# Spreading the last tokens and v over the DMA engines, row sums on the full array, and unread products in gaps

## The chip, the cores and the metric

The kernel runs on one core of a Trainium2 chip. The metric is the time of one execution on the device in microseconds (us), the median of several runs. The core has a matrix engine (TensorE, PE in the profile; its weight loads are listed apart as PEld), VectorE (DVE), ScalarE (ACT), GpSimd (POOL), a sync engine (SP) that issues most transfers, and 16 DMA engines that carry them out.

## The reference

Attention over keys and values that are averaged in groups of eight, and a mixing MLP on its output. Sizes: 8 batches, 8 heads, 576 tokens, 64 values per head; so the model width is 512 and there are 72 pooled keys; the hidden width is 2048.

```python
k_p = k.reshape(B, H, 72, 8, 64).mean(axis=3)
v_p = v.reshape(B, H, 72, 8, 64).mean(axis=3)
attn = softmax(q @ k_p.T / 8)                     # 576 x 72 for each batch and head
x = heads side by side of (attn @ v_p)            # B x 576 x 512

a1 = alpha1 * x + beta1
u = x + lam * einsum('ts,bsd->btd', w_tok, a1)    # mixes tokens
a2 = alpha2 * u + beta2
out = u + lam * (maximum(a2 @ w_ch1, 0) @ w_ch2)
```

The 576 tokens are four chunks of 128 and a rest of 64, called rem below. Because alpha1, beta1 and lam don't depend on the token, beta1 enters the mix as lam * beta1 times the sum of each row of w_tok; the kernel computes these row sums and puts them into one extra row of the transposed w_tok.

## The kernel before

The work is one program in which every engine has its own queue of instructions in the order written. A start computes batch 0's attention and mix; then come nine blocks of 512 tokens of the MLP, with the attention and mix of the next batch woven between their matmuls.

The loads. A rem transfer brings two rows of 64 values for 128 partitions, from four heads (every second one) times 32 pairs of tokens:

```python
def load_rem(b, queue=nc.sync):
    raw = work.tile([P, 2, 2, 2, D], FP, tag="rem_raw", bufs=2, name="rem_raw")
    for i, src in enumerate((q, k)):
        for h in range(2):
            queue.dma_start(
                out=raw[:, i, h].rearrange("p c d -> p (c d)"),
                in_=src[b, h::2, 512:576, :].rearrange("a (i c) d -> a i (c d)", c=2))

def load_v(b, hp):
    v_hp = work.tile([SPG, 2, 8, D], FP, tag="v_hp", bufs=4, name="v_hp")      # SPG = 72
    nc.sync.dma_start(out=v_hp.rearrange("g h p d -> g h (p d)"),
                      in_=v[b, 2 * hp:2 * hp + 2].rearrange("h (g p) d -> g h (p d)", p=8))
```

The transposed w_tok and its row sums. The last of the five products of a row sum has only 64 rows:

```python
def setup_wtok(tcx, copy):
    ...                                        # five transposes on PE
    copy(out=wtT[:, 0:5, P * tcx:P * tcx + trc], in_=...)      # ScalarE

def setup_rowsum(tcx):
    ...
    for sc in range(5):
        kk = P if sc < 4 else 64
        nc.tensor.matmul(out=ps[:, 0:trc], lhsT=ones_bf[0:kk], rhs=wtT[0:kk, sc, cols],
                         start=(sc == 0), stop=(sc == 4))
    nc.scalar.copy(out=wtT[64:65, 4, cols], in_=ps[64:65, 0:trc])
```

Helpers that the order below names:

```python
def setup_vectors():       # one transpose of beta2, and a copy by ScalarE
def setup_bias(g):         # 16 products of w_ch1 with beta2, one column each, and a copy by ScalarE
def keep_warm(count):      # products that nothing reads
    ps = gp("ps_warm")
    for _ in range(count):
        nc.tensor.matmul(out=ps, lhsT=identity_bf, rhs=warm)
def mix_T(b, c, eng):      # 5 products of 512 columns, then u = x + product (VectorE),
                           # then u_bf = u * alpha2 (VectorE or GpSimd)
def mix_uT(key):           # 4 transposes of u_bf on PE, then a copy by ScalarE to u_fm
def mlp_A(n, j):           # 4 products of w_ch1 with u_fm, then relu by ScalarE
```

The start of the program, cut (att_F transposes q, att_K pools k on PE, att_V sums v on VectorE, S are scores and exponentials, AV the products with v, att_X scales x for the mix):

```python
load_qk(0, 0)
...                        # small vectors on ScalarE's queue: lam, alpha1, alpha2, beta1, lam, beta2
load_v(0, 0)
load_qk(0, 2)
load_rem(0)
load_v(0, 2)
load_qk(0, 1); load_v(0, 1); load_qk(0, 3); load_v(0, 3)
...
broadcast(0, lam_bc)       # one row to 128 partitions, a float32 product on PE
sum_k(0, 0, nc.gpsimd)
cast_q(0, 0, nc.vector.tensor_copy)
att_F(0, 0)
broadcast(1, lamal_bc, by=lam_bc)
att_V(0, 0)
sum_k(0, 2, nc.gpsimd)
cast_q(0, 2, nc.scalar.copy)
nc.vector.tensor_tensor(out=lamb1, in0=b1row, in1=lamrow, op=ALU.mult)
att_F(0, 2)
...
broadcast(2, al2_bc)
cast_rem(0, nc.gpsimd, nc.vector.tensor_copy)
att_Frem(0, (0,), nc.vector.tensor_copy)
att_K(0, 0, nc.vector.tensor_copy)
att_V(0, 2)
pro_S(0)
pro_S(2)
...                        # w_tok, w_ch1 and w_ch2 are loaded; the other two pairs of heads
setup_wtok(0, nc.scalar.copy)
setup_wtok(1, nc.scalar.copy)
att_X(0, 2, 4, eng=nc.gpsimd)
pro_AV(3)
setup_wtok(2, nc.scalar.copy)
setup_rowsum(0)
setup_rowsum(1)
setup_wtok(3, nc.scalar.copy)
att_X(0, 6, 8)
setup_rowsum(2)
setup_rowsum(3)
mix_T(0, 0, nc.gpsimd)
mix_T(0, 1)
mix_T(0, 2, nc.gpsimd)
mix_uT((0, 0))
mix_T(0, 3)
mix_uT((0, 1))
...                        # loads of batch 1
setup_vectors()
setup_bias(0)
mix_uT((0, 2))
keep_warm(1)
mix_uT((0, 3))
...                        # blocks: mlp_A, mlp_B, and the next batch between
```

Of the kernel before, what the change touches and what calls it, by code (L numbers as in the profile page):

```python
# [9 lines left out]
BF = mybir.dt.bfloat16  # L10
AF = mybir.ActivationFunctionType
ALU = mybir.AluOpType
AX = mybir.AxisListType

P = 128
# [8 lines left out]
def kernel(  # L24
# [59 lines left out]
# [4 lines that stand above are left out]
            for h in range(2):  # L88
                queue.dma_start(
                    out=raw[:, i, h].rearrange("p c d -> p (c d)"),  # L90
                    in_=src[b, h::2, 512:576, :].rearrange("a (i c) d -> a i (c d)", c=2))
        st1[b]["rem_raw"] = raw

    def load_v(b, hp):
        v_hp = work.tile([SPG, 2, 8, D], FP, tag="v_hp", bufs=4, name="v_hp")
        nc.sync.dma_start(out=v_hp.rearrange("g h p d -> g h (p d)"),
                          in_=v[b, 2 * hp:2 * hp + 2].rearrange("h (g p) d -> g h (p d)", p=8))
        st1[b]["v"][hp] = v_hp

    def cast_rem(b, eng, copy=None):  # L100
        raw = st1[b]["rem_raw"]
        rq = work.tile([P, 2, 2, D], BF, tag="rem_q", bufs=2, name="rem_q")
        rk = work.tile([P, 2, D], BF, tag="rem_k", bufs=2, name="rem_k")
        (copy or eng.tensor_copy)(out=rq.rearrange("p c h d -> p h c d"), in_=raw[:, 0])  # L104
        eng.tensor_tensor(out=rk, in0=raw[:, 1, :, 0], in1=raw[:, 1, :, 1], op=ALU.add)
        st1[b]["rem"] = rq, rk
# [45 lines left out]
    for t, src in ((b1row, moe_beta1), (lamrow, moe_lam)):  # L152
# [16 lines left out]
    ones_bf = const.tile([P, P], BF, tag="ones_bf", name="ones_bf")  # L169
    nc.vector.memset(identity_bf, 0.0)  # L170
    nc.vector.memset(pool_main, 0.125)
    nc.vector.memset(pool_rem, 0.125)
    nc.vector.memset(identity, 0.0)
    nc.gpsimd.affine_select(out=identity_bf, in_=identity_bf, compare_op=ALU.not_equal,
                            fill=1.0, base=0, pattern=[[-1, P]], channel_multiplier=1)
    for t, n, width in ((pool_main, 64, 2), (pool_rem, 32, 4)):
        nc.gpsimd.affine_select(out=t, in_=t, compare_op=ALU.is_ge, fill=0.0, base=0,
                                pattern=[[-width, n]], channel_multiplier=1)
        nc.gpsimd.affine_select(out=t, in_=t, compare_op=ALU.is_ge, fill=0.0, base=width - 1,
                                pattern=[[width, n]], channel_multiplier=-1)  # L180
    nc.gpsimd.affine_select(out=identity, in_=identity, compare_op=ALU.not_equal,
                            fill=1.0, base=0, pattern=[[-1, P]], channel_multiplier=1)
    nc.vector.memset(ones_bf, 1.0)

    vp1_pool, kpT_pool, ET_pool = [], [], []
    for i in range(4):
# [18 lines left out]

    wtT = const.tile([P, 6, 640], BF, tag="wtT", name="wtT")
    nc.vector.memset(wtT[:, :, S:640], 0.0)

    def broadcast(i, out, by=None):

        ps = gp("ps_bc")
        nc.tensor.matmul(out=ps, lhsT=ones_row, rhs=vecs[:, i])
        if by is None:
            nc.scalar.copy(out=out, in_=ps)
        else:
            nc.vector.tensor_tensor(out=out, in0=by, in1=ps, op=ALU.mult)
# [6 lines left out]
    def setup_wtok(tcx, copy):  # L223

        trc = P if tcx < 4 else REM
        w = wt_bf[0:trc, S * tcx:S * tcx + 640]
        strided = w[:, 0:512].rearrange("p (m c) -> p c m", c=4)
        ps_w = gp("ps_w").bitcast(BF)
        for sc in range(5):
            nc.tensor.transpose(out=ps_w[0:P, trc * sc:trc * sc + trc],  # L230
                                in_=strided[:, sc, :] if sc < 4 else w[:, 512:640],
                                identity=identity_bf[0:trc, 0:trc])
        copy(out=wtT[:, 0:5, P * tcx:P * tcx + trc],
             in_=ps_w[:, 0:5 * trc].rearrange("p (s t) -> p s t", t=trc))

    def setup_rowsum(tcx):

        trc = P if tcx < 4 else REM
        cols = slice(P * tcx, P * tcx + trc)
        ps = gp("ps_rs")  # L240
        for sc in range(5):
            kk = P if sc < 4 else 64
            nc.tensor.matmul(out=ps[:, 0:trc], lhsT=ones_bf[0:kk], rhs=wtT[0:kk, sc, cols],
                             start=(sc == 0), stop=(sc == 4))
        nc.scalar.copy(out=wtT[64:65, 4, cols], in_=ps[64:65, 0:trc])

    def setup_wtok_odd():
# [56 lines left out]
    def att_Frem(b, us, copy):  # L304

        st = st1[b]
        if "ps_qr" not in st:
            ps_q = gp("ps_qr").bitcast(BF)
            for c in range(2):
                nc.tensor.transpose(out=ps_q[:, 128 * c:128 * c + 128],  # L310
                                    in_=st["rem"][0][:, c].rearrange("p h d -> p (h d)"),
                                    identity=identity_bf)
            st["ps_qr"] = ps_q
        for u in us:
            copy(out=st["qT"][u][:, 512:640].rearrange("p (r i c) -> p r c i", r=2, c=2),
                 in_=st["ps_qr"][:, 0:256].rearrange("p (c r u i) -> p u r c i", c=2, r=2,
                                                     u=2)[:, u])

    def att_K(b, u, copy):

        st = st1[b]
        ps_kp = gp("ps_kp")
        kp = ps_kp[:, 0:2 * SPG].rearrange("p (r g) -> p r g", g=SPG)
        for r in range(2):
            nc.tensor.matmul(out=kp[:, r, 0:64],
                             lhsT=st["k"][u + 2 * r].rearrange("p h d -> p (h d)"), rhs=pool_main)
        nc.tensor.matmul(out=kp[:, :, 64:72], lhsT=st["rem"][1].rearrange("p h d -> p (h d)"),  # L327
                         rhs=pool_rem.rearrange("p (r u g) -> p u r g", u=2, g=8)[:, u])
        for hh in range(2):
            rows = slice(64 * hh, 64 * hh + 64)  # L330
            copy(out=kpT_pool[u][rows, hh], in_=kp[rows])  # L331
# [44 lines left out]
    def att_X(b, h0, h1, groups=1, eng=nc.vector):  # L376

        x, xs = st1[b]["x"], xs_pool[b % 2]
        for h in range(h0, h0 + 4 * groups, 4):
            cols = slice(D * h, D * (h + h1 - h0))  # L380
            eng.tensor_tensor(  # L381
                out=xs[:, 0:4, cols], in0=x[:, 0:4, cols],
                in1=lamal_bc[:, cols].unsqueeze(1).to_broadcast((P, 4, D * (h1 - h0))),
                op=ALU.mult)
        p0 = 64 * (b % 2)
        for h in range(h0, h0 + 4 * groups, 4):
            cols = slice(D * h, D * (h + h1 - h0))
            eng.tensor_tensor(out=xs[p0:p0 + 64, 4, cols], in0=x[p0:p0 + 64, 4, cols],  # L388
                                    in1=lamal_bc[p0:p0 + 64, cols], op=ALU.mult)
# [20 lines left out]
    def mix_T(b, c, eng=nc.vector):  # L410
        key, s = chunk_of(b, c)
        p0, p1 = (0, P) if c < 4 else (64 * (b % 2), 64 * (b % 2) + 64)
        xs = xs_pool[b % 2]
        ps_tok = gp("ps_tok")
        t0 = P * c - 64 * (b % 2) if c == 4 else P * c
        for sc in range(5):
            kk, at = (P, sc) if sc < 4 else (P, 5) if b % 2 else (65, 4)
            nc.tensor.matmul(out=ps_tok, lhsT=wtT[0:kk, at, t0:t0 + P],  # L418
                             rhs=xs[0:kk, sc, :], start=(sc == 0), stop=(sc == 4))
        nc.vector.tensor_tensor(out=s["u"][p0:p1, :], in0=st1[b]["x"][p0:p1, c, :],  # L420
                                in1=ps_tok[p0:p1, 0:DM], op=ALU.add)
        eng.tensor_tensor(out=s["u_bf"][p0:p1, :], in0=s["u"][p0:p1, :],  # L422
                          in1=al2_bc[p0:p1, :], op=ALU.mult)
# [54 lines left out]
    def pro_AV(hp):  # L478
        att_AV(0, 2 * hp)
        att_AV(0, 2 * hp + 1)  # L480
# [12 lines left out]
    for i, p0 in ((0, 64), (1, 0)):  # L493
        nc.scalar.copy(out=xs_pool[i][p0:p0 + 1, 4, :], in_=lamb1[p0:p0 + 1, :])
    broadcast(2, al2_bc)
    cast_rem(0, nc.gpsimd, nc.vector.tensor_copy)
    att_Frem(0, (0,), nc.vector.tensor_copy)
    att_K(0, 0, nc.vector.tensor_copy)
# [27 lines left out]
    setup_wtok(0, nc.scalar.copy)  # L526
    setup_wtok(1, nc.scalar.copy)
    att_X(0, 2, 4, eng=nc.gpsimd)
    pro_AV(3)
    setup_wtok(2, nc.scalar.copy)  # L530
    setup_rowsum(0)
    setup_rowsum(1)
    setup_wtok(3, nc.scalar.copy)
    att_X(0, 6, 8)
    setup_rowsum(2)
    setup_rowsum(3)
    mix_T(0, 0, nc.gpsimd)
    mix_T(0, 1)
    mix_T(0, 2, nc.gpsimd)
    mix_uT((0, 0))  # L540
    mix_T(0, 3)
# [6 lines left out]
    for hp in (1, 3):  # L548
        load_qk(1, hp)
        load_v(1, hp)  # L550
    setup_vectors()
    setup_bias(0)
    mix_uT((0, 2))
    keep_warm(1)
    mix_uT((0, 3))


    def attention(b):
# [89 lines left out]
```

The softmax here doesn't subtract the row's maximum and nothing guards it: scores larger than these inputs give would overflow.

## Time and profile before

| what | value |
|---|---|
| time, median of 3 runs | 385.42 us (384.75 to 386.6) |
| profiled execution | span 384.7 us, 5969 instructions |
| data moved | 43.01 MB in 34307 packets |
| sync queue, share of 16 DMA engines | 34.7% |
| v, per transfer | 288 KB, 32 transfers |
| q, k, per transfer | 256 KB, 32 transfers each |
| rem of q and of k, per transfer | 64 KB, 16 transfers each |
| w_tok | 576 KB and 72 KB as kept, landed 5.8 and 6.0 us after issue |
| first score product | 14.97 us |
| first mix product | 31.98 us |
| first large MLP product | 41.10 us |

The page of a profile lists busy times of the engines, then the span in 40 equal slices (each digit the busy share in tenths), the DMA queues, and the chain of work that ended last, followed back from the end. Finer answers from the same trace are used below: the chain of waits in order of time (start, length, what), the instructions of one engine in order of time (start, length, engine and line, operation, operands, how many, and in brackets the idle time before and what ended it), and stretches of time with the busy time of every engine. L89 is line 89 of the kernel.

### The profile page before, as it was taken

To read this page: it belongs to the slowest core of one execution; us is meant where nothing else is said; L and a number is where in the kernel's file an instruction comes from. 1 tells how busy PE (TensorE), PEld (TensorE's weight loads), DVE (VectorE), ACT (ScalarE), POOL (GpSimd) and SP (SyncE) were. 2 spreads that over 40 slices of the span, in tenths; PEclk is the share of its full clock that TensorE was granted. 3 is DMA by queue.
4 is the path that set the end of the run, shared out by engine and by line. 5 is a ranking of instruction groups with operands and counts; after the bars stand their busy time and mean duration, and the time that the engine had idled before them with its cause. 6 is when DMAs were issued, how large, how long until landed. Compare 5 with 4: busy or idle time off the path is not lost.

```text
span 384.7 us, 5969 instructions
## 1 busy us (share of the span) xinstructions
PE 358.4 (93%) x2221; PEld 193.9 (50%) x2263; DVE 219.0 (57%) x464; ACT 191.2 (50%) x383; POOL 81.8 (21%) x133
## 2 busy tenths in 40 slices
PE   6579899879999999999999999999999999999995
PEld 2265455435554555445545554455555544544542
DVE  6394809975577457755776578637863685011011
ACT  3462468416951595148605860487138713722710
POOL 4372246610350044004400360035000000000000
PEclk9999899999999999999999999999999999999999
DMA  5799995803951195118511861076110001002012
GB/s 154 212 176 216 220 243 147 250 28 120 223 137 57 57 238 130 55 45 219 162 55 36 229 163 54 30 213 173 41 54 1 23 34 55 1 27 83 0 42 67
DMA packets 34307, 43.01 MB, mean 112 GB/s; under 512 B 2331, under 2 KB 23903, under 8 KB 34278
## 3 DMA queue, kind: packets, MB, share of 16 engines
q1 hardware_dynamic: 31872, 37.76, 34.7%
q0 software_dynamic: 2384, 4.86, 6.8%
q8 instruction: 17, 0.28, 0.3%
q14 instruction: 12, 0.10, 0.1%
q10 hardware_dynamic: 22, 0.02, 0.0%
HBM read 38.04 MB, written 9.44 MB: 123 GB/s over the span
## 4 chain that ended last, share of the span: by engine, by line
PE 79%; DVE 14%; DMA 3%; ACT 2%; issue 1%; SPq 1%; POOL 0%; ACTq 0%; POOLq 0%
PE ps_h L444 33%; PE ps_ch L460 23%; PE ps_tok L418 12%; DVE x_tm L373 4%; DVE xs L381 3%; PE ps_sc L349 3%; PE ps_uT L433 2%; PE ps_q L297 2%; DMA v_hp<-in_v_dram 1%; DMA rem_raw<-in_k_dram 1%; PE ps_av L365 1%; DVE xs L388 1%; DVE rec L371 1%; DVE u_sb L465 1%; ACT ET L351 1%
## 5 line engine op out<-in xcount | busy, mean ns | idle before, releaser
L460 PE MATMUL ps_ch<-w,Hj 128*128 128x512 bf16 x555 | 137.8, 379 | 1.0
L444 PE MATMUL ps_h<-u_fm,w 128*128 128x512 bf16 x558 | 132.6, 383 | 1.7 <-ACT u_fm L435 0.7
L447 ACT ACTIVATE Hj<-ps_h,bias_cols 128x512 bf16<-128x512 f32 x144 | 99.1, 689 | 41.6 <-PE ps_h L444 41.2
L444 PEld LDWEIGHTS <-w 128*128 128x128 bf16 x576 | 63.6, 115 | 52.8 <-issue 3.1
L460 PEld LDWEIGHTS <-Hj 128*128 128x128 bf16 x576 | 54.4, 98 | 48.9
L435 ACT COPY u_fm<-ps_uT 128x512 bf16<-128x512 bf16 x36 | 21.0, 586 | 95.9 <-PE ps_uT L433 95.8
L351 ACT ACTIVATE ET<-ps_sc 72x288 f16<-72x288 f32 x128 | 44.6, 405 | 25.9 <-PE ps_sc L349 25.2
L418 PE MATMUL ps_tok<-xs,wtT 128*128 128x512 bf16 (+1 forms) x197 | 50.3, 386 | 4.1 <-DVE xs L381 3.7
L465 DVE TENSOR_TENSOR u_sb<-u_sb,ps_ch 128x512 f32<-128x512 f32 x36 | 24.5, 682 | 50.6 <-PE ps_ch L460 50.2
L420 DVE TENSOR_TENSOR u_sb<-x_tm,ps_tok 128x512 f32<-128x512 f32 (+1 forms) x40 | 27.5, 687 | 39.0 <-PE ps_tok L418 38.0
L337 DVE TENSOR_TENSOR v_hp<-v_hp 72x512 f32<-72x512 f32 x64 | 37.0, 578 | 1.9 <-DMA v_hp<-in_v_dram 0.3
L331 DVE CAST kpT<-ps_kp 64x144 bf16<-64x144 f32 x30 | 9.1, 305 | 43.9 <-PE ps_kp L327 43.6
L418 PEld LDWEIGHTS <-wtT 128*128 128x128 bf16 (+1 forms) x200 | 19.3, 100 | 28.0 <-issue 4.1
L373 DVE TENSOR_TENSOR x_tm<-ps_av,rec 128x320 f32<-128x320 f32 x64 | 31.5, 492 | 2.2
L349 PE MATMUL ps_sc<-qT,kpT 128*72 128x288 bf16 x128 | 27.6, 308 | 1.9 <-DVE x_tm L373 1.2
L118 POOL TENSOR_TENSOR qk_raw<-qk_raw 128x256 f32<-128x256 f32 x32 | 24.6, 769 | 19.2 <-DMA qk_raw<-in_k_dram 15.7
L422 DVE TENSOR_TENSOR u_bf<-u_sb,al_bc 128x512 bf16<-128x512 f32 (+1 forms) x38 | 26.4, 695 | 1.5
L104 POOL CAST rem_q<-rem_raw 128x256 bf16<-128x256 f32 x7 | 2.8, 397 | 105.7 <-DMA rem_raw<-in_q_dram 105.7
L111 POOL CAST q_bf<-qk_raw 128x512 bf16<-128x512 f32 x28 | 17.9, 640 | 33.1 <-DMA qk_raw<-in_q_dram 23.1
L365 PEld LDWEIGHTS <-ET 72*128 72x128 f16 x256 | 16.9, 102 | 14.4 <-issue 1.3
L381 DVE TENSOR_TENSOR xs<-x_tm,lamal_bc 128x512 bf16<-128x512 f32 x31 | 22.3, 721 | 1.0
L371 DVE RECIPROCAL rec<-ps_av 128x5 f32<-128x5 f32 x64 | 12.1, 189 | 15.9 <-PE ps_av L369 15.5
(88 smaller groups left out, 248.5 us busy)
## 6 DMA issues: line engine op xcount, KB each, us to landing
v_hp<-in_v_dram SPq DMA_DIRECT2D x32, 288.0 KB
qk_raw<-in_q_dram SPq DMA_DIRECT2D x32, 256.0 KB
qk_raw<-in_k_dram SPq DMA_DIRECT2D x32, 256.0 KB
out_dram<-u_sb SPq DMA_DIRECT2D x32, 256.0 KB
w<-in_moe_w_ch_dram POOLq DMA_DIRECT2D x6, 512.0 KB, 15.0
rem_raw<-in_q_dram SPq DMA_DIRECT2D x16, 64.0 KB
rem_raw<-in_k_dram SPq DMA_DIRECT2D x16, 64.0 KB
w<-in_moe_w_ch_dram POOLq DMA_DIRECT2D x1, 1024.0 KB, 12.3
```

The costliest lines, as they stand in the source:

```text
L337: nc.vector.tensor_tensor(out=t[:, :, 0:n], in0=t[:, :, 0:n], in1=t[:, :, n:2 * n], op=ALU.add)
L349: nc.tensor.matmul(out=ps_sc[0:SPG, 0:288], lhsT=kpT_pool[u][:, hh, r, :], rhs=st["qT"][u][:, S * r + n0:S * r + n0 + 288])
L351: nc.scalar.activation(out=ET[:, 64 + n0:64 + n0 + 288], in_=ps_sc[0:SPG, 0:288], func=AF.Exp, bias=0.0, scale=0.125)
L373: nc.vector.tensor_tensor(out=x[:, :, dd:dd + D], in0=av[:, :, 0:64], in1=rec.unsqueeze(2).to_broadcast((P, 5, D)), op=ALU.mult)
L381: eng.tensor_tensor(out=xs[:, 0:4, cols], in0=x[:, 0:4, cols], in1=lamal_bc[:, cols].unsqueeze(1).to_broadcast((P, 4, D * (h1 - h0))), op= ...
L418: nc.tensor.matmul(out=ps_tok, lhsT=wtT[0:kk, at, t0:t0 + P], rhs=xs[0:kk, sc, :], start=(sc == 0), stop=(sc == 4))
L420: nc.vector.tensor_tensor(out=s["u"][p0:p1, :], in0=st1[b]["x"][p0:p1, c, :], in1=ps_tok[p0:p1, 0:DM], op=ALU.add)
L422: eng.tensor_tensor(out=s["u_bf"][p0:p1, :], in0=s["u"][p0:p1, :], in1=al2_bc[p0:p1, :], op=ALU.mult)
L444: nc.tensor.matmul(out=ps_h, lhsT=w1_of(cc, j), rhs=u_fm[n][:, cc, :], start=(cc == 0), stop=(cc == 3))
L447: nc.scalar.activation(out=t, in_=ps_h, func=AF.Relu, bias=bias_cols[:, j:j + 1], scale=1.0)
L460: nc.tensor.matmul(out=ps, lhsT=Hj[n, j][:, 128 * m:128 * m + 128], rhs=w2[:, j, :], start=(j == 0), stop=(j == NJ - 1))
L465: nc.vector.tensor_tensor(out=u, in0=u, in1=ps, op=ALU.add)
```

## The change

It has four parts.

1. The rows of rem are put on partitions with the pair of tokens outermost and the head inside, so that the memory side of the transfer begins with 32 rather than 4. The patterns that read rem's transposes and pool its keys follow; the pooling matrix is now made by one select into a wider tile and a reduction. The 72 rows of v come as 64 and 8. The purpose is that transfers use all DMA engines.
2. The last product of a row sum takes all 128 rows, with a matrix whose lower half is zero, so that no product uses half of the array.
3. setup_vectors, setup_bias(0) and the row sums stand at other places of the start.
4. Ten more unread products stand in the start: three before the last transposes of w_tok, and eight in place of one around the last transposes of u. They are meant to keep the matrix engine occupied where it would wait.

```diff
@@ load_rem
-                    in_=src[b, h::2, 512:576, :].rearrange("a (i c) d -> a i (c d)", c=2))
+                    in_=src[b, h::2, 512:576, :].rearrange("a (i c) d -> i a (c d)", c=2))
@@ load_v
-        nc.sync.dma_start(out=v_hp.rearrange("g h p d -> g h (p d)"),
-                          in_=v[b, 2 * hp:2 * hp + 2].rearrange("h (g p) d -> g h (p d)", p=8))
+        for g0, g1 in ((0, 64), (64, SPG)):
+            nc.sync.dma_start(
+                out=v_hp[g0:g1].rearrange("g h p d -> g h (p d)"),
+                in_=v[b, 2 * hp:2 * hp + 2, 8 * g0:8 * g1].rearrange("h (g p) d -> g h (p d)", p=8))
@@ constants
-    nc.vector.memset(pool_rem, 0.125)
+    pool_each = const.tile([P, 32, 4], BF, tag="pool_each", name="pool_each")
+    nc.vector.memset(pool_each, 0.0)
-    for t, n, width in ((pool_main, 64, 2), (pool_rem, 32, 4)):
+    for t, n, width in ((pool_main, 64, 2),):
 ...
+    each4 = pool_each.rearrange("p (g a) j -> p g a j", a=4)
+    nc.gpsimd.affine_select(out=each4, in_=each4, compare_op=ALU.not_equal, fill=0.125,
+                            base=0, pattern=[[-16, 8], [-1, 4], [-4, 4]], channel_multiplier=1)
+    ones_lo = const.tile([P, P], BF, tag="ones_lo", name="ones_lo")
+    nc.vector.memset(ones_lo[0:64], 1.0)
+    nc.vector.memset(ones_lo[64:128], 0.0)
 ...
+    nc.vector.tensor_reduce(out=pool_rem, in_=pool_each, op=ALU.max, axis=AX.X)
@@ setup_rowsum
-            kk = P if sc < 4 else 64
-            nc.tensor.matmul(out=ps[:, 0:trc], lhsT=ones_bf[0:kk], rhs=wtT[0:kk, sc, cols],
-                             start=(sc == 0), stop=(sc == 4))
+            nc.tensor.matmul(out=ps[:, 0:trc], lhsT=ones_bf if sc < 4 else ones_lo,
+                             rhs=wtT[:, sc, cols], start=(sc == 0), stop=(sc == 4))
@@ att_Frem, att_K
-                 in_=st["ps_qr"][:, 0:256].rearrange("p (c r u i) -> p u r c i", c=2, r=2, u=2)[:, u])
+                 in_=st["ps_qr"][:, 0:256].rearrange("p (c i r u) -> p u r c i", c=2, r=2, u=2)[:, u])
-                         rhs=pool_rem.rearrange("p (r u g) -> p u r g", u=2, g=8)[:, u])
+                         rhs=pool_rem.rearrange("p (g r u) -> p u r g", r=2, u=2)[:, u])
@@ the start
     broadcast(2, al2_bc)
+    setup_vectors()
     cast_rem(0, nc.gpsimd, nc.vector.tensor_copy)
 ...
     att_X(0, 2, 4, eng=nc.gpsimd)
+    setup_rowsum(0)
     pro_AV(3)
     setup_wtok(2, nc.scalar.copy)
-    setup_rowsum(0)
     setup_rowsum(1)
+    setup_bias(0)
+    keep_warm(3)
+    att_X(0, 6, 8)
     setup_wtok(3, nc.scalar.copy)
-    att_X(0, 6, 8)
+    mix_T(0, 0, nc.gpsimd)
     setup_rowsum(2)
+    mix_T(0, 1)
     setup_rowsum(3)
-    mix_T(0, 0, nc.gpsimd)
-    mix_T(0, 1)
     mix_T(0, 2, nc.gpsimd)
     mix_uT((0, 0))
     mix_T(0, 3)
 ...
-    setup_vectors()
-    setup_bias(0)
+    keep_warm(3)
     mix_uT((0, 2))
-    keep_warm(1)
+    keep_warm(2)
     mix_uT((0, 3))
+    keep_warm(3)
```

More of the change, by code (lines that the diff above doesn't have):

```diff
@@ L315, in att_Frem @@
             copy(out=st["qT"][u][:, 512:640].rearrange("p (r i c) -> p r c i", r=2, c=2),
-                 in_=st["ps_qr"][:, 0:256].rearrange("p (c r u i) -> p u r c i", c=2, r=2,
+                 in_=st["ps_qr"][:, 0:256].rearrange("p (c i r u) -> p u r c i", c=2, r=2,
                                                      u=2)[:, u])
```

## The prediction

> **What bounds the kernel now.** I read the page first: shares, slices, then the chain.
>
> ```profile
> PE 358.4 (93%) x2221; PEld 193.9 (50%) x2263; DVE 219.0 (57%) x464; ACT 191.2 (50%) x383; POOL 81.8 (21%) x133
> ...
> PE   6579899879999999999999999999999999999995
> ...
> DMA  5799995803951195118511861076110001002012
> ...
> PE 79%; DVE 14%; DMA 3%; ACT 2%; issue 1%; SPq 1%; POOL 0%; ACTq 0%; POOLq 0%
> ```
>
> One slice is 9.6 us. From the third slice on PE is nearly always busy, apart from one dip near 75 us, and only 3% of the chain is DMA. A change that touches loads and set-up products can therefore gain only in the first 45 us or so; from 84 us on, loads wait in the sync queue behind output stores and have slack. So I followed the chain of waits over the first 60 us, in order of time (start, length, what):
>
> ```profile
> 1.81 5.39 DMA v_hp<-in_v_dram
> 7.21 0.02 issue
> 7.22 0.56 SPq L89
> ...
> 8.39 5.34 DMA rem_raw<-in_k_dram
> ...
> 13.87 0.47 POOL rem_k L105
> ...
> 14.38 0.21 PE ps_kp L327
> ...
> 15.46 2.49 ACT ET L351 x8
> ```
>
> The first scores wait for the k rows of the last 64 tokens, a 64 KB transfer that takes 5.34 us, as long as 288 KB of v. Before it, the sync queue itself stands: in the program each transfer waits for one that went out up to eight issues earlier, and the second rem issue waits for v. Fine stretches of time (start:end and length, then busy us of PE, PEld, DVE, ACT, POOL, then clock, DMA share, GB/s):
>
> ```profile
> 8.00:9.00 1.00, 0.61 (x5) 0.42 (x5) 0.93 (x3) 0.33 (x1) 0.48 (x1) 1.00 0.12 34
> 9.00:10.00 1.00, 1.00 (x2) 0.42 (x2) 1.00 (x2) 0.59 (x1) 0.92 (x2) 1.00 0.24 73
> 11.00:12.00 1.00, 0.43 (x4) 0.27 (x4) 0.30 (x1) 1.00 (x2) 0.00 (x0) 1.00 0.94 287
> ```
>
> While the rem transfers are alone, the 16 DMA engines are 12 to 24% busy, at 34 to 73 GB/s; two us later 287 GB/s flow. 0.24 is about 4 of 16 engines.
>
> Then the timeline of PE's weight loads in the row sums:
>
> ```profile
> 28.09 0.47 PEld L243 LDWEIGHTS <-ones_bf 128*128 128x128 bf16 x4
> 28.75 0.56 PEld L243 LDWEIGHTS <-ones_bf 64*128 64x128 bf16 x5 [0.20 <-issue]
> 29.51 0.10 PEld L243 LDWEIGHTS <-ones_bf 64*128 64x128 bf16 x1 [0.20 <-issue]
> ```
>
> Ahead of each 64-row load PE's loader stands 0.20 us. Ten matmuls of two row sums take 1.40 us in the chain. Last, the clock, in stretches of 3.41 us:
>
> ```profile
> 38.07:41.48 3.41, 2.10 (x30) 1.60 (x29) 3.38 (x4) 1.89 (x5) 1.01 (x1) 1.00 1.05 211
> 41.48:44.89 3.41, 3.30 (x8) 1.21 (x8) 3.41 (x3) 1.19 (x2) 0.00 (x0) 0.50 1.04 247
> ```
>
> In the first, PE waits for the transposed u and does one-column bias products (2.10 of 3.41 us busy); in the next its clock is halved, exactly where the first large products start: 8 matmuls instead of some 16.
>
> **What the Trainium skill says, and whether the trace agrees.**
> - "DMA: Bandwidth & Descriptors", "Why a DMA increments its semaphore by 16 and not by 1": the engines used are the largest number up to 16 that divides the slowest dimensions of both sides. Then q and k (128 rows) use 16, v (72) 12, rem (4 heads outermost) 4. The 0.24 agrees for rem.
> - "TensorEngine Tiling (Array Packing)", "Key Properties": a change of tiling mode drains TensorE; the 0.20 us beside each 64-row load agrees.
> - "TensorE: Matmul & The Clock Gate", "The HAM clock gate": activity over free-running windows of about 3.4 us halves or restores the clock. The 0.50 window of 3.41 us agrees. The printed 1.00 before it does not show the cold start: the mixing matmuls' weight loads at 32.38 and 32.81 us are 0.43 us apart, against 0.22 later (16 in 3.48 us), so PE is at half speed until about 34.5 us.
>
> **The change, part by part.**
>
> *Row order of rem, v in two pieces.* Estimated bytes per DMA engine for batch 0, from the skill's rule. Before, the four busiest: q and k 8 x 16 KB, v 4 x 24 KB, rem 4 x 16 KB = 288 KB. The k of the last pair reaches GpSimd at 20.45 us; with a start near 2 us this is 15.7 KB/us on those engines. After, the 64-row v piece uses 16 engines and the 8-row piece 8: 8 x 16 + 4 x (16 + 4) + 4 x 4 = 224 KB, so 14.3 us at that rate, and loads end about 4 us earlier. The cost: 32 more issues of some 0.5 us on the sync queue, and the waits on earlier transfers fall otherwise: the second q now waits for the first (about 3.8 us instead of an issue at 2.38), and ScalarE's b2row issue for v's large piece (about 5.8 us instead of 5.06). By sequence I put the last rem transfer at 9.5 us, against 13.73. But other work then ends last: three float32 broadcasts of 2.07 us on PE, the second ending at 7.06 and the third at 11.0; v's sums, lamb and rem_q on VectorE up to 10.7; and VectorE's head grows by two memsets and a reduction, about 0.45 us by the 0.10 to 0.17 us steps of its neighbours, which delays the first q cast (4.04) and all behind it. So: transposes of rem at 11.3, pooled k at 11.5, the first of its two copies by 12.4, so the first score at 12.4 instead of 14.97. **Gain 2.5 us**, not 4.2, and it is kept: exponentials, q casts and VectorE's divisions follow in the same order, and later data arrive 4 us earlier.
>
> *Row sums on the full array.* Five 128-column matmuls cost about 0.53 us at half clock (ten transposes took 1.07) against 0.70 to 0.80: about 0.15 to 0.2 each, five times, **0.9 us**, of which I count 0.8.
>
> *Order and filling before the mix.* Added ahead of the first mix: four bias columns, 0.74 us, and three unread products, 3 x 0.43 = 1.28 us at half clock. Moved behind it: row sums 2 and 3, with the 0.5 us in which PE waited for ScalarE's copy. From the first w_tok transpose to the mix the sequence is 1.4 (copy) + 0.53 + 0.55 + 0.53 + 0.53 + 0.74 + 1.28 + 0.53 = 6.1 us, against 31.98 - 26.05 = 5.9; the two row sums then add 0.6 to 1.0 inside the mix. Net of the row-sum gain: **a loss of about 0.9 us**, which includes that gain.
>
> *The gap before the first large product.* b2row's transposition with its copy (0.6 us stall) and the bias products (0.74) leave this place. The way is now: mix product, add 0.69, scale 0.7 to 0.9, transposition 0.25, copy 0.59. The last of the four mix products ends at 38.0 in the old count, so the first large product comes at 40.6, not 41.10: **0.5 us**. The eight unread products (seven more than before, 1.7 us at full clock) fit into that gap of 2.6 us.
>
> *Clock.* If the gap is full, the halving at 41.5 does not come: 15 matmuls took 5.30 us, at 0.216 they need 3.24: 2.06 us in this profile. The profiled run is the slowest of the three (386.6; the others 385.42 and 384.75), so the median may carry less; I count **1.3 us**. And the first rise of the clock may come earlier, since dense work starts about 1.5 us earlier relative to the mix: half of it, **0.8 us**.
>
> Sum: 2.5 - 0.9 + 0.5 + 1.3 + 0.8 = 4.2, and 0.2 for the fifth row sum and steadier loads of batch 1: 4.4 us. 385.4 - 4.4 = **381.0 us**. From 45 us on I expect a parallel shift: the dip at 75 us is VectorE's chain (2.15 us wait for xs), whose start hangs on PE.
>
> **Rivals.**
> 1. *The load was hidden; the broadcasts bind.* PE's third broadcast ends at 11.0 before, and nothing shortens it; if the q of the second pair, now issued 1.5 us later, also comes later (cast at 7.72), the third broadcast slides and the gain falls to 1 us. Against: fewer bytes per engine lie ahead of it. Time 382.5 to 383.
> 2. *The filling costs more than the clock.* If the bias columns wait for the first quarter of w1 (it lands 5.7 us or more after its issue at 21.64, so before 29; used at 26.05 + 3.5 = 29.6 in the old count, 27.1 with the shift), PE stands before the mix. For: it is in order, and w1 follows k's last sums. Against: that issue moves earlier too. Then 383 to 384.
> 3. *The sync queue becomes the bound.* Twice as many v issues and waits on small transfers could starve the engines in the first 12 us; then rem lands at 12 and it is 383. Against: about 20 issues of 0.5 us are done by 12 us while data need until 16.
> 4. *Everything follows the data.* If the start loses all 4.2 us and the clock gives 2.1 and 1.3: 377.5 to 378.
>
> **Range and chances.** Rivals 1 to 3 set the upper end, rival 4 the lower: 378.3 to 383.8. A gain over 2% needs less than 377.7 us, more than every term at its full size; a loss over 2% needs 393.1 us, for which no term is large enough.
>
> **What will show it.** Rem_k's DMA near 9.5 us and no stretch at 12 to 24% DMA before 12 us; first score at 12.0 to 12.9 us; no 0.20 us ahead of row-sum loads; first large product near 38.2 us (41.1 - 2.5 + 0.9 - 0.5 - 0.8); clock 1.00 in all later stretches; later blocks as long as before (39 us). I am wrong if the clock still drops after the mix, if PE waits for w1 in the bias products, or if the later blocks change.

## The result, and the profile after

| | median of the runs | range |
|---|---|---|
| before, same series | 385.09 us (4 runs) | 383.9 to 386.6 |
| after | 389.94 us (4 runs) | 389.27 to 391.09 |
| after / before | 1.0127 | 95% interval 1.0083 to 1.0171 |

The change costs 1.3%. The prediction was 381.0 us, with 378.3 to 383.8 as its range: the time lies 6 us above the range, and the sign is wrong.

The page of after, in the same parts as before (engine shares, 40 slices of 9.7 us for PE, its clock and the DMA engines, and the engines' shares of the chain that ended last):

```profile
PE 357.9 (92%) x2231; PEld 194.0 (50%) x2273; DVE 221.7 (57%) x467; ACT 190.8 (49%) x383; POOL 85.7 (22%) x132
...
PE   6664999879999999999999999999999999999995
PEclk9995999999999999999999999999999999999999
DMA  6999687723761176116611761167110011002002
...
PE 75%; DVE 14%; DMA 6%; issue 2%; SPq 2%; POOL 1%; ACT 0%; DVEq 0%; ACTq 0%
```

PE works as long as before (357.9 us, 358.4 then), in a longer span. What differs sits in one place: the fourth slice (29 to 39 us) has PE at 4 tenths and the clock at 5 tenths, where before had 9 and 9. The clock's line of before:

```profile
PEclk9999899999999999999999999999999999999999
```

In the chain DMA has doubled, from 3% to 6%. The chain of waits in order of time (start, length, what) names the transfer:

```profile
20.07 1.48 POOL w L276 x2
21.55 12.36 DMA w<-in_moe_w_ch_dram
33.91 0.14 issue
34.04 0.63 PE ps_bias L296 x15
...
45.89 3.62 PE ps_h L455 x16
```

The load of w_ch1 (the kernel's w1), issued as three transfers by GpSimd, is now a link of 12.36 us, and a bias product is released by it. PE's timeline shows how long it stood (start, length, line, operands, count; in brackets the idle time before and its releaser):

```profile
26.64 0.17 PE L296 MATMUL ps_bias<-b2c_bf,w 128*128 128x1 bf16 x1
34.04 0.63 PE L296 MATMUL ps_bias<-b2c_bf,w 128*128 128x1 bf16 x15 [7.24 <-DMA w<-in_moe_w_ch_dram]
```

One bias product runs at 26.64 us; the second waits 7.24 us. Stretches of 3.41 us around it (busy us of PE, PEld, DVE, ACT, POOL, then clock, DMA share, GB/s):

```profile
29.56:32.97 3.41, 0.00 (x0) 0.00 (x0) 0.00 (x0) 0.00 (x0) 0.00 (x0) 0.50 1.13 215
32.97:36.38 3.41, 2.12 (x23) 1.54 (x25) 0.00 (x0) 0.16 (x1) 0.00 (x0) 0.50 1.08 216
36.38:39.80 3.42, 3.42 (x14) 1.52 (x12) 0.69 (x1) 0.95 (x2) 0.28 (x1) 0.50 1.06 212
39.80:43.20 3.40, 3.40 (x25) 1.83 (x23) 1.98 (x3) 0.84 (x2) 1.35 (x2) 1.00 0.82 164
```

For one stretch no compute engine does anything; the DMA engines are fully used. The clock is halved for three stretches, two of them with PE at work again, so the mix starts slowly too.

The landmarks, before and after: first score 14.97 and 12.11 us (2.86 earlier), first large MLP product 41.10 and 45.89 (4.79 later), the mix of batch 1 79.28 and 82.59 (3.3 later), span 384.7 and 387.5 (2.8 later). The medians differ by more, 4.85, because the profiled execution of before was its longest (386.57 us) and that of after its shortest (389.27). So the loads do what they should, and between 12 and 46 us 7.65 us are lost. Of these 2 come back by the end, 1.5 of them in the first block, where before's clock was halved for one stretch (41.48 to 44.89 us, the last line of the prediction's views) and after's was not.

### The profile page after: what moved, and what is told of

The parts are those of the page before. It is cut to its first block, busy times and chain, and to the rows that moved or that the text cites. A ratio compares the mean times of both kernels' runs of the same rounds, so it can differ in the third digit from the quotient of the medians.

```text
span 387.5 us, 6062 instructions
## 1 busy us (share of the span) xinstructions
PE 357.9 (92%) x2231; PEld 194.0 (50%) x2273; DVE 221.7 (57%) x467; ACT 190.8 (49%) x383; POOL 85.7 (22%) x132
## 3 DMA queue, kind: packets, MB, share of 16 engines
q1 hardware_dynamic: 32640, 37.76, 34.5%
## 4 chain that ended last, share of the span: by engine, by line
PE 75%; DVE 14%; DMA 6%; issue 2%; SPq 2%; POOL 1%; ACT 0%; DVEq 0%; ACTq 0%
PE ps_h L455 31%; PE ps_ch L471 23%; PE ps_tok L429 12%; DVE x_tm L384 3%; DMA w<-in_moe_w_ch_dram 3%; DVE xs L392 3%; PE ps_sc L360 2%; PE ps_uT L444 2%; DMA qk_raw<-in_k_dram 2%; PE ps_q L308 1%; DVE v_hp L348 1%; DVE xs L399 1%; DVE u_sb L476 1%; DVE rec L382 1%; PE ps_av L376 1%
## 5 line engine op out<-in xcount | busy, mean ns | idle before, releaser
L348 DVE TENSOR_TENSOR v_hp<-v_hp 72x512 f32<-72x512 f32 x64 | 37.9, 593 | 1.6
L121 POOL TENSOR_TENSOR qk_raw<-qk_raw 128x256 f32<-128x256 f32 x32 | 27.6, 861 | 16.4 <-DMA qk_raw<-in_k_dram 11.7
L114 POOL CAST q_bf<-qk_raw 128x512 bf16<-128x512 f32 x28 | 19.9, 709 | 48.9 <-DMA qk_raw<-in_q_dram 33.7
```

Of the source, the lines that this page charges most:

```text
L121: eng.tensor_tensor(out=raw[:, :, 0:2], in0=raw[:, :, 0:2], in1=raw[:, :, 2:4], op=ALU.add)
L348: nc.vector.tensor_tensor(out=t[:, :, 0:n], in0=t[:, :, 0:n], in1=t[:, :, n:2 * n], op=ALU.add)
```

## The experiments

Three readings of that wait were open. The profile's line says "DMA w", which the prediction had seen as a danger for the first of the three transfers only. **Theory A**: the products, which read columns 0 to 511 of w1, wait for all three transfers, and everything else about the change is roughly as predicted. **Theory B**: the first transfer itself is late, because the faster loads and the other weights now share the DMA engines with it; then the loads are at fault and moving the products helps no more than in part. **Theory C**: all of w1 comes later because of the new loads, so that the products would wait at their old place too. The program's list of instructions on PE shows which transfers an instruction waits for (2, 3 and 4 are w1's three transfers in order; other waits cut out):

```
after, one tile w1 of 2048 columns         w1 as three tiles
Ldweights w   waits transfer 2             Ldweights w_0   waits transfer 2
Matmult   ps_bias                          Matmult   ps_bias
Ldweights w   waits transfers 4 and 3      Ldweights w_0
Matmult   ps_bias                          Matmult   ps_bias
...           14 more pairs, no wait       ...             14 more pairs, no wait
                                           Ldweights w_1   waits transfer 3  (next group of columns)
```

With one tile the second weight load waits for the transfers of columns 512 to 2047, though it reads none of them. The list of before has the same waits. A transfer into w1[:, :, 0:512] is four pieces in the tile, 2048 columns apart. My reading of the list is that the dependency tracking takes such a transfer as one span from its first to its last element. That fits both loads: the first reads the first of the four pieces, which lies ahead of the spans of the other two transfers, and waits for neither; the second reads the next piece, which lies inside both. But the list shows the waits, not their reason.

**The bias products back at their old place.** After, with this one edit:

```diff
-    setup_bias(0)
     keep_warm(3)
     att_X(0, 6, 8)
 ...                        # the mix, loads of batch 1
+    setup_bias(0)
     keep_warm(3)
     mix_uT((0, 2))
```

> The changed kernel with the first four bias columns moved back behind the loads of batch 1. Theory A (in the changed kernel PE stands 7.2 us in the early bias products, whose second weight load waits for all of w1): the wait falls to at most 1 us, the first mix product comes near 28 us instead of 36.3, the first large product near 37, and the time is 379 to 382 us. Theory B (the loss lies in more and smaller transfers on the sync queue and in later blocks): the time stays at 388 to 391 us. Theory C (w1 itself comes later because of the new loads): PE stands some 5 us at the bias products' new place, 386 to 388 us.

Measured: 381.81 us (380.02 to 384.48, 20 runs) against 386.2 of before in the same series (71 runs): 0.9894 (0.9867 to 0.9921). The bias wait shrinks to 0.65 us at 34.41, the first mix product comes at 28.26, the first large one at 37.26. One helper moved by 7 us of program decides between 1.3% slower and 1.1% faster.

**w1 as three tiles.** The products stay early; only what they wait for changes. After, with:

```diff
-    w1 = const.tile([P, 4, DFF], BF, tag="w1", name="w1")
+    w1 = [const.tile([P, 4, n], BF, tag=f"w1_{i}", name=f"w1_{i}")
+          for i, n in enumerate((512, 512, 1024))]
```

and the two places that address it.

> The changed kernel with w1 kept in three tiles, one for each of its three transfers; nothing else moves. Theory A: the early bias products then wait for the first transfer alone, which lands 6.3 us after its issue at 20.0, so PE goes on at 26.6 or a little later; the wait of 7.2 us is gone, the clock, which rose at 26.2 us in the changed kernel, stays up, and the time is 378 to 381 us. Theory C (the first quarter itself is late, at about 34 us): the wait of 7 us stays, 389 to 390 us. Theory B: 388 to 391 us.

Measured: 382.13 us (380.88 to 384.43, 20 runs), 0.9911 (0.9885 to 0.9937). PE's timeline of this kernel, same columns as above:

```profile
26.94 0.70 PE L298 MATMUL ps_bias<-b2c_bf,w 128*128 128x1 bf16 x16
...
29.27 1.96 PE L431 MATMUL ps_tok<-xs,wtT 128*128 128x512 bf16 x5
```

All 16 bias products run without a wait at 26.94 us, so the transfer that they read was there: theory B falls. In after that first transfer landed 6.3 us after its issue at 20.0, the last one 12.36 us after its issue at 21.55. The smallest, median and largest landing of the three, from the source view of the issuing line, in before and then in after, hardly differ, which speaks against theories B and C at once:

```profile
DMA to landing us min/median/max: 5.7/7.5/12.3
```

```profile
DMA to landing us min/median/max: 6.3/8.3/12.4
```

20.0 + 6.3 is 26.3 us, just ahead of the first bias product at 26.64; 21.55 + 12.36 is 33.91, just ahead of the second at 34.04. Against after, this kernel is ahead by 8.05 us at the first large product (37.84 against 45.89), by 8.06 at the mix of batch 1 (74.53 against 82.59) and by 8.0 at the end (379.5 against 387.5), so the loss is carried to the end unchanged. Of it 7.24 us are the wait; the other 0.8 I put down to the slow clock behind it.

**The early bias products alone, in the kernel before.** The reverse test: before, with setup_vectors and setup_bias(0) at after's places and nothing else.

```diff
     broadcast(2, al2_bc)
+    setup_vectors()
 ...
     setup_rowsum(1)
+    setup_bias(0)
     setup_wtok(3, nc.scalar.copy)
 ...
-    setup_vectors()
-    setup_bias(0)
     mix_uT((0, 2))
```

> The kernel before with nothing but beta2's transposition and the first four bias columns moved to their early places. Theory A (the early bias products wait for all of w1, whatever the loads are): PE reaches them near 29 us and stands until w1's last transfer lands near 35.5 us, so 6 to 6.5 us; the first large product comes 4 to 5 us later than 41.1, and the time is 4 to 6 us above the kernel before. Theory C (it took the new loads to make w1 late): no wait over 1 us, time within 1 us of the kernel before.

Measured: 394.08 us (392.15 to 395.74, 4 runs) against 387.46 (7 runs): 1.0174 (1.0114 to 1.0234). PE's timeline:

```profile
29.86 0.20 PE L285 MATMUL ps_bias<-b2c_bf,w 128*128 128x1 bf16 x1
37.45 0.63 PE L285 MATMUL ps_bias<-b2c_bf,w 128*128 128x1 bf16 x15 [7.39 <-DMA w<-in_moe_w_ch_dram]
```

The same wait (7.39 us), and again a halved clock for 10.24 us from 32.91. So this one move makes the loss without any other part of the change, and theory C falls: with the old loads the wait is as long. Wait, delay and loss are all larger than expected: the first large product comes at 49.09, 8 us later than in before, and the median is 6.6 us above.

**The loads.** Three kernels: before with both row orders (rem and v), before with rem's alone, and the three-tile kernel with both undone. Their edits are the hunks load_rem, constants, att_Frem, att_K and load_v of the change's diff; the smallest of them, for v:

```diff
-        for g0, g1 in ((0, 64), (64, SPG)):
-            nc.sync.dma_start(out=v_hp[g0:g1]..., in_=v[..., 8 * g0:8 * g1]...)
+        nc.sync.dma_start(out=v_hp..., in_=v[...]...)
```

> The kernel before with part 1 of the change alone (rem's row order with what follows from it, v as 64 and 8 rows). Theory A: the first score comes at 12.1 us instead of 15.0, all later work of the start moves by 2.5 to 3 us, but the bias products after the mix then reach w1's last transfer (33.9 us in the changed kernel) about when it lands, which costs up to 1 us: 382.0 to 383.5 us. Theory B (these loads are what costs): 386 us or more.

> The kernel before with rem's row order alone, v in one transfer. If rem is what mattered: the first score near 12.5 us and a gain of 2 to 2.5 us, as with both parts of the loads (2.3 us). If the pieces of v are half of it: 1 to 1.3 us.

> The changed kernel with w1 in three tiles and rem and v loaded as before: order, row sums and unread products without part 1. Theory A: first score at 15.0 us again, no wait in the bias products, clock up before the first large product: 3 us slower than the changed kernel with three tiles, 381 to 383.5 us. If order and unread products cost as much as they give: 385 us.

| kernel | median (runs) | ratio to before | first score | first large | mix of batch 1 |
|---|---|---|---|---|---|
| before + rem and v | 383.8 (20) | 0.9941 (0.9916 to 0.9967) | 11.95 | 38.37 | 76.23 |
| before + rem | 383.03 (20) | 0.9942 (0.9915 to 0.9968) | 12.37 | 37.19 | 75.72 |
| three tiles, old loads | 386.01 (20) | 0.9991 (0.9963 to 1.0018) | 15.49 | 42.86 | 79.85 |

The second kernel's median is from another series, in which before had 385.55 us (the first and third: 386.2), so compare the ratios. They leave out the few executions that fell in a slower state of the chip, three of the 20 with old loads; the medians do not.

Rem's row order is worth 0.6% alone, and without the new loads the rest of the change (with w1 in three tiles) is worth nothing that the interval shows. There the expected 381 to 383.5 us was missed; the other reading, that order and unread products cost as much as they give, is the nearer one. The mix starts at 33.99 us, 2 us later than in before, and the bias products do wait, 0.86 us, now for the first transfer of w1. v in two pieces adds nothing measurable: 0.9941 with, 0.9942 without. The three-tile kernel with v in one transfer says the same:

> The changed kernel with w1 in three tiles and v in one transfer of 72 rows again. If the two pieces matter: [...]the last k of batch 0 comes 1 us later, and the time is 0.5 to 1 us above 382.1. If rem's row order alone is what helps, the second q is issued without a wait and fewer issues are made: 381.5 to 382.5.

Measured: 381.66 us (4 runs), 0.9866 (0.981 to 0.9922); first score at 12.71.

**The unread products.** The three-tile kernel without the three early ones (first), and with only one late one as in before, so one in place of eleven (second):

```diff
-    keep_warm(3)            # ahead of the last w_tok transposes: both kernels
 ...
-    keep_warm(3)            # the second kernel only
     mix_uT((0, 2))
-    keep_warm(2)
+    keep_warm(1)
     mix_uT((0, 3))
-    keep_warm(3)
```

> The changed kernel with w1 in three tiles, and without the three unread products ahead of the mix. If those cost what they last (1.3 us at half clock) and the clock rises at the same time anyway: 1 us under the 382.1 us with them. If they are what lifts the clock a window (3.4 us) earlier: the same or up to 1 us slower.

> The changed kernel with w1 in three tiles, with one unread product as in the kernel before instead of eleven. If the eight in the gap keep the clock up: the clock shows a stretch of 0.50 after the first large product and the time is 1 to 2 us above 382.1. If moving the bias products out of the gap has already shortened it enough, the clock stays at 1.00 and the time is 380.5 to 382.

Measured, 4 runs each: 382.39 us, 0.988 (0.9824 to 0.9936), and 382.53 us, 0.9862 (0.98 to 0.9925); the three-tile kernel with all eleven has 0.9911 (0.9885 to 0.9937). Neither a benefit nor a cost of the ten products is seen: the differences of 1 and of 1 to 2 us that the two expectations name can't be told apart in these intervals. The clock rises near 25.8 us in both, without the early three. With one in place of eleven the first large product comes at 35.78, 2 us earlier, at full clock; but later, from 73.72 to 77.14 us, that kernel's clock is halved in the pause before the mix of batch 1.

**The row sums.** The three-tile kernel with the last product of each row sum on 64 rows again:

```diff
-                             lhsT=ones_bf if sc < 4 else ones_lo, rhs=wtT[:, sc, cols]
+                             lhsT=ones_bf[0:kk], rhs=wtT[0:kk, sc, cols]      # kk = 64 for sc = 4
```

> The changed kernel with w1 in three tiles, and the last product of each row sum with 64 rows again. If the half array costs what the gaps of 0.20 us say: 0.15 to 0.2 us for each of five row sums, 0.8 us in all, of which up to half hides behind ScalarE's copies: 0.3 to 0.8 us above the same kernel with full products. If it costs nothing: the same within 0.3 us.

Measured: 382.99 us (16 runs), 0.9927 (0.9903 to 0.9952), against 0.9911 with full rows: not told apart. The trace does show the mechanism. PE's weight loads, here and then in after, both at half clock:

```profile
27.09 0.47 PEld L255 LDWEIGHTS <-ones_bf 128*128 128x128 bf16 x4
27.75 0.10 PEld L255 LDWEIGHTS <-ones_bf 64*128 64x128 bf16 x1 [0.20 <-issue]
```

```profile
24.96 0.32 PEld L254 LDWEIGHTS <-ones_bf 128*128 128x128 bf16 x3 [0.41 <-issue]
25.24 0.15 PEld L254 LDWEIGHTS <-ones_lo 128*128 128x128 bf16 x1
```

The 0.20 us is back with 64 rows and gone with 128; five of them, 1 us at most, drown in the interval of 1 us either way.

**The pause near 75 us.** Every variant pauses before the mix of batch 1, where PE waits for VectorE's scaled x (xs): 2.1 us in before and after, 1.8 in the three-tile kernel. VectorE does a 2.3 us scaling of w_ch2 in that block (at 61.28 us in before), ahead of batch 1's pooled k; I moved the fourth of these scalings ahead of the last mix product of batch 0:

```diff
-        todo.append((5.0 + 3 * g, lambda g=g: scale_w2(g)))
+        todo.append((5.0 + 1.9 * g, lambda g=g: scale_w2(g)))
```

> The changed kernel with w1 in three tiles, and VectorE's fourth scaling of w2 (2.28 us, now inside batch 1's attention) moved ahead of the last mix product of batch 0, where VectorE idles 9 us; PE's order is untouched. If the dip before batch 1's mix is VectorE's chain: its start to the mix takes 22.05 - 2.28 = 19.8 us, PE's wait for xs of 1.8 us goes, and the time is 1.5 to 2.5 us under 382.1. If late data or PE's own work set the dip: less than 0.5 us.

Measured: 380.61 us (380.45 to 381.06, 4 runs), 0.9871 (0.9836 to 0.9907). The expected end of the wait did not come. PE's waits from 60 to 80 us, summed (what waited, for what, total, times, longest):

```profile
PE ps_tok L431 <- DVE xs L394: 2.5, 1, 2.5
PE ps_kp L338 <- POOL k_bf L122: 1.1, 1, 1.1
```

and on VectorE's timeline of that kernel:

```profile
57.91 1.14 DVE L350 TENSOR_TENSOR v_hp<-v_hp 72x512 f32<-72x512 f32 x2 [0.61 <-DMA v_hp<-in_v_dram]
...
62.22 0.64 DVE L344 CAST kpT<-ps_kp 64x144 bf16<-64x144 f32 x2 [0.67 <-PE ps_kp L340]
```

VectorE, relieved, now waits itself: for v of batch 1 and, through PE, for k on GpSimd. So the scaling alone was not what held the pause. Whether the variant beats the three-tile kernel the overlapping intervals leave open.

**All that helped or did no harm, together.** Three tiles of w1, v in one transfer, one unread product, the fourth scaling early:

> All that seemed to help: the changed kernel with w1 in three tiles, v in one transfer, one unread product instead of eleven, and the early fourth scaling. If the parts add up: 378 to 380 us, and no stretch of half clock near 75 us because the dip is filled. If the dip is set by batch 1's data: 381 to 382 us and the clock drops near 75 us.

Measured: 379.42 us (378.73 to 381.41, 4 runs) against 385.55 (35 runs): 0.9847 (0.9802 to 0.9892). It has the lowest median of all versions and beats both kernels. But its interval overlaps those of most other three-tile variants, so that the parts add up is not shown. In the profiled execution the clock is full from 25.9 us to the end (mean granted clock 1.000), but in the other three the mean is 0.994 to 0.997, so there it dropped somewhere. PE still waits 1.87 us for xs:

```profile
72.62 1.24 PE L429 MATMUL ps_tok<-xs,wtT 128*128 128x512 bf16 x5 [1.87 <-DVE xs L392]
```

## Why the prediction was wrong, point by point

**The step that failed** is in "Order and filling before the mix": "Added ahead of the first mix: four bias columns, 0.74 us". It counted work and no wait. The place was named, in rival 2 and in "I am wrong if ... PE waits for w1 in the bias products", but rival 2 asked when the *first quarter* of w1 lands. That quarter was in time (landed 26.3, wanted 26.64; rival 2 had said 27.1). The program waits for all of w1, which landed at 33.91: a term of +7.24 us where the sum had none. The page before could not show this, because there the products ran at 39 us, when all three transfers were in; the list of instructions and their waits would have, before any run.

The work of that stretch was sized well. The prediction had 6.1 us from the first w_tok transpose to the mix. In after it is 12.84 us (23.46 to 36.30), and 5.6 without the wait; in the three-tile kernel, 5.93 (23.34 to 29.27). One small reading was low: the wait for ScalarE's copy, counted as 0.5 us, is 0.8 in before's waits.

**Clock, "1.3" and "0.8".** The late halving at 41.5 us does vanish in after, worth most of the 1.5 us that it regains in the first block. But after the 7.24 us of idle PE the clock is halved from 29.56 to 39.80 us. Against the three-tile kernel, which itself ran its mix at half clock until 30.7, that leaves about 0.8 us (8.05 minus 7.24). And the reason given for the gain, that unread products fill the gap, was not shown: with one in all instead of eleven the clock also stayed up there (first large product at 35.78), and so it did in before with both new loads and its single unread product. With rem's alone it was halved (37.66 to 41.08). One profile each, so I take it that where the clock's stretches happen to fall matters as much as the filling; what moves them stays open. The size was too large as well, because it came from one profile. The mean granted clock is recorded for every execution: on average 0.9948 in before (71 executions), 0.9959 with three tiles and 0.9965 with the bias products late (20 each). If the whole missing share is lost time, my estimate from these figures and the time of 386 us is that 0.4 to 0.7 us less is lost to half clock, where the prediction counted 1.3. In these figures the start at half speed is not seen, as the prediction notes.

**Row order of rem, v in two pieces: right mechanism, right size.** "First score at 12.4", "gain 2.5 us, not 4.2": 12.11 and 2.86. Rem's k reaches GpSimd at 9.87 us ("9.5"). The rows of rem carry it; the part given to v was worth nothing measurable, and the argument by bytes on the busiest DMA engines, 288 against 224 KB, is not supported by a run for v's share.

**Row sums, 0.9 us.** The 0.20 us gaps vanish as said. Their worth in time is not resolved.

**"From 45 us on I expect a parallel shift."** Between after and the three-tile kernel it holds to 0.1 us. Against before it does not hold for every variant. From the first large product to the mix of batch 1: before 38.18 (of which some 2 are its halved clock), three tiles 36.69, before with the loads 37.86 and with no halved clock. There PE waits 4.7 us for VectorE in the block (2.5 for x, 2.2 for xs), in before 3.3 (1.2 and 2.1). Part of the reason may be that the next batch's work on GpSimd doesn't start earlier by as much as PE does. Its first q cast of batch 1, in before and then with the bias products late, where PE is 3.84 us ahead:

```profile
46.26 0.61 POOL L111 CAST q_bf<-qk_raw 128x512 bf16<-128x512 f32 x1 [7.18 <-DVE w L274]
```

```profile
44.97 0.61 POOL L114 CAST q_bf<-qk_raw 128x512 bf16<-128x512 f32 x1 [10.63 <-DMA qk_raw<-in_q_dram]
```

It starts 1.29 us earlier. In before a scaling on VectorE released it, here q's transfer did, and the DMA engines are at 0.99 of their time from 40 to 50 us. That late data set the pause is argued from these lines and from the scaling experiment; no run isolates it.

**Without the failed step** the total stands: the three-tile kernel is 0.9911 of before, 382.0 us on the 385.42 of the prediction, inside its range and 1 us above its centre; its first large product comes at 37.84 where 38.2 was said. That does not confirm each term. The loads' 2.5 us is shown (0.9941, or 2.3 us). The other terms summed to 1.9 us; the ratios leave 1.2 us for them with the new loads and 0.3 without, with intervals of about 1 us either way on each ratio.

"A loss over 2% ..., for which no term is large enough" had the same gap: taken alone, the missing term cost 1.7% (1.0114 to 1.0234), which has 2% in its interval.

## What to carry to other kernels

When a reader is moved ahead, look up in the instruction list what it waits for, not only what it reads: here 512 columns waited for all 2048, since all transfers went into one tile, and a wait that costs nothing at the old place (all data in) costs 7 us at the new. A tile that arrives in several transfers is better several tiles before its readers are moved between them. And an engine that executes in order should not have anything that needs late data put ahead of work whose data are there.

## What the runs showed of the hardware

The clock can rise without filling. In after it rises near 26.1 us, before any unread product, as PE's weight loads show: ten start 0.10 us apart from 23.41, the four of a row sum 0.055 us apart from 26.30:

```profile
23.41 1.04 PEld L242 LDWEIGHTS <-wt_bf 128*128 128x128 bf16 x10
...
26.30 0.27 PEld L254 LDWEIGHTS <-ones_bf 128*128 128x128 bf16 x4
26.52 0.10 PEld L254 LDWEIGHTS <-ones_lo 128*128 128x128 bf16 x1
```

That is some 8.4 us before it did in the kernel before (34.5). It rises at about 25.8 us in the two kernels without early unread products, on transposes, row sums and products with v alone. In the three-tile kernel, with three early unread products, it rose only at 30.7. After 7.24 us of idle PE the clock stays halved for three stretches of 3.41 us, the second with 2.12 us of work in it and the third full; the Trainium skill, "TensorE: Matmul & The Clock Gate", "The HAM clock gate", lets such windows both lower and restore it, and the trace agrees with windows of 3.41 us. The page speaks of an idle window, but here a window with work in it was enough, at a pause of little over 2 us: with the bias products late, PE was busy 1.25 of 3.41 us before the mix of batch 1, and the next stretch ran at half clock. With the early scaling a pause as long (2.50 us) did not halve it.

```profile
71.72:75.13 3.41, 1.25 (x6) 0.49 (x5) 3.26 (x7) 0.00 (x0) 2.82 (x5) 1.00 0.24 75
75.13:78.54 3.41, 3.19 (x8) 1.17 (x8) 1.28 (x4) 0.00 (x0) 0.00 (x0) 0.50 0.00 0
```

VectorE and GpSimd can slow each other where they work at once, though not equally. With the bias products late, GpSimd's cast of q at 54.78 us took 2.80 us instead of 0.61 beside a scaling on VectorE, which took its usual 2.28 us. In before a sum of k at 61.29 took 2.58 us instead of 0.46 beside the same scaling. Two sums of v took 1.71 us instead of 1.14 beside GpSimd's sums of k, one of which took 0.79 instead of 0.46. The first and the third case:

```profile
54.78 2.80 POOL L114 CAST q_bf<-qk_raw 128x512 bf16<-128x512 f32 x1 [1.79 <-DMA qk_raw<-in_q_dram]
...
57.70 1.71 DVE L348 TENSOR_TENSOR v_hp<-v_hp 72x512 f32<-72x512 f32 x2
```
